# A gated MLP's first pair: both batches' gates first, then the second batch's values directly and the first batch's by Strassen

## The chip, the cores and the metric

The kernel runs on one core of a Trainium2 chip. The metric is the device time of one execution in microseconds. The engines of the core are TensorE (PE; its weight loads are PEld), VectorE (DVE), ScalarE (ACT), GpSimd (POOL) and SyncE (SP), whose queue issues the loads. Each works through its own instructions in order, and semaphores hold one back until another has finished.

## The reference

Clustered attention gives `x` of 1536 tokens (two batches of 768) by 512 features. Two MLPs follow. The change lies in the first sixth of the second one, which has 1536 hidden features:

```python
def _moe_ref(x, w_in, w_out):            # first MLP, 2048 hidden features
    h = x @ w_in
    g = h * (1.0 / (1.0 + np.exp(-h)))
    return (g @ w_out).astype(np.float32)

def _moe2_ref(x, w_gate, w_val, w_out):  # second MLP, 1536 hidden features
    gate = 1.0 / (1.0 + np.exp(-(x @ w_gate)))
    val = x @ w_val
    return (gate * val @ w_out).astype(np.float32)
```

## The kernel before, in words

Every float32 product is made of three matmuls: an operand is split into a high part (ScalarE's `cast`, L62) and the rest (a subtraction, L74, L617 or L769), and high times high, high times low and low times high are summed in PSUM.

**Pairs.** The first MLP runs over 8 pairs of 128-column blocks of its hidden features, the second over 6 (`N2`). For a pair the first product (`w_gate`, `w_val`) is a 2 by 2 block product over halves of the 512 input features and halves of a batch's tokens. `direct` (L779) computes it with 48 matmuls of 128x384 for one batch and one of the two weights. `strassen` (L714) needs seven block products of 6 matmuls each, in the order x, y, z, w, X, v, W, so 42; but it needs sums of weights (`seven`, with the four steps L644 to L647 on GpSimd) and sums of the operand `y` (`sums`: L88, L91, L95 and L99 on VectorE, each with a cast L62 and a subtraction L74), and it combines the products with additions on VectorE (L737, L739, L747, L753, L756).

**Weights.** `converted` (L600 to L609) loads a weight of 64-bit floats into a raw buffer (two in turn, `rp`) and makes it float32 in five steps: ScalarE L605, GpSimd L606, VectorE L607, L608, L609. `weights` starts the conversion two jobs ahead of its use. A raw buffer is free for the load two further on when the last of its steps, L609, has ended. Raw tiles are named `rg`, `rv`, `ru` (gate, value, out), converted ones `cg`, `cv`, `cu`, with pair and half behind (`cv1_0`).

**PSUM.** Banks come from two pools of two buffers, `ppa` and `ppb`. `direct` takes one of each for its two halves `m`, `strassen` takes `ppa` for x and w and `ppb` for y, z and v. A third bank of one pool has to wait until the first has been read.

**Order.** TensorE's order is that of the code (`tc.manual_schedule`). The orders of VectorE, ScalarE and GpSimd come from a scheduler that has the whole program before it, under the limits of `tc.issue_after`.

**The place of the change.** After the first MLP's last product (`mixed`, L829) the first pair of the second MLP is computed directly for both batches, so that Strassen's sums of `y` can be made beside it: `gated_directly(0, 0)` has the gates q and the values r of batch 0, then come the sums of batch 0, `gated_directly(0, 1)`, and the sums of batch 1. `gate` applies the sigmoid on ScalarE (L861), `value` multiplies on VectorE (L865), and `split` casts the result on ScalarE (`ghb`, L62) and subtracts on VectorE (`glb`, L769). Then `out_of(0)` (L887) multiplies pair 0 by `w_out` in six steps of two 128-token blocks and ScalarE copies each bank away (L807). `gated(1, ALL)` follows, by Strassen for both batches at once.

Of the kernel before, what the change touches and what calls it, by code (L numbers as in the profile page):

```python
# [31 lines left out]
def clustered_attention_then_two_mlps(ctx, tc, qT, kT, v, cen, w1i, w1o, w2g, w2v, w2o, out):  # L32
# [633 lines left out]
    def job(key, make, *args):  # L666
        place[key] = len(jobs)
        jobs.append(partial(make, *args))

    def flat(w):  # L670
        return w.rearrange("p k c -> p (k c)")
# [4 lines left out]
            job(("1o", i, e), plain, w1o[i, e], f"o{i}_{e}")  # L676
    for i in range(N2):
        job(("2g", i), seven if i else four, [flat(w2g[2 * i + n]) for n in range(2)], f"g{i}")
        job(("2v", i), seven if i else four, [flat(w2v[2 * i + n]) for n in range(2)], f"v{i}")
        for k in range(2):  # L680
            job(("2o", i, k), plain, flat(w2o[2 * i + k]), f"u{i}_{k}")

# [20 lines left out]
    def temporary(name):  # L703
        return up.tile([P, 2, HS], F32, tag="u", name=name)
# [57 lines left out]
    def split(src, m, at, i, subber):  # L762

        for t in "hl":
            if (i, m, t) not in gs:
                gs[i, m, t] = gp.tile([P, 2, B, HS], R32, tag=f"g{t}{m}", name=f"g{t}{i}_{m}")
        hi, lo = (gs[i, m, t][(slice(None), *at)] for t in "hl")
        cast(nc.scalar, hi, src)
        subber.tensor_tensor(lo, src, hi, op=ALU.subtract)  # L769

    def direct(w, name, take, b):

        for m in range(2):
            o = bank(f"{name}_{b}{m}", (ppa, ppb)[m])
            for h in range(2):
                for r in range(2):
                    for k in range(KQ):
                        for n, (s, t) in enumerate(((0, 0), (0, 1), (1, 0))):
                            nc.tensor.matmul(  # L779
                                o[:, h, 0:HS],  # L780
                                lhsT=w[f"a{m + 1}{r + 1}"][s][:, k, :],
                                rhs=right[b, f"{r + 1}{h + 1}"][t][:, k, :],
                                start=r == 0 and k == 0 and n == 0,
                                stop=r == 1 and k == KQ - 1 and n == 2,
                            )
            take(o[:, :, 0:HS], m, b)
            yield
# [65 lines left out]
        yield from strassen(weights("2g", i), f"g{i}", gate, bs)  # L853
        yield from strassen(weights("2v", i), f"v{i}", value, bs)

    def gated_directly(i, b):
        gates = {}

        def gate(c, m, b):
            gates[m] = temporary(f"g2{i}_{m}_{b}")  # L860
            nc.scalar.activation(gates[m], c, AF.Sigmoid)  # L861

        def value(c, m, b):
            g = gates[m]
            nc.vector.tensor_tensor(g, c, g, op=ALU.mult)  # L865
            split(g, m, (slice(0, 2), b), f"b{i}", nc.vector)

        yield from direct(weights("2g", i), f"q{i}", gate, b)
        yield from direct(weights("2v", i), f"r{i}", value, b)

    oa = acc.rearrange("p d h b s -> p (d h b s)")
    PER = HS // P
# [1 line left out]
    def out_of(i):  # L874
# [1 line left out]
        half = B * S // P // 2  # L876
        pairs = [(t, t + 1) for t in range(0, 2 * half, 2)]
        if i == 0:
            ts = [t for b in range(B) for t in range(2 * half) if t % half // PER == b]
            pairs = [tuple(ts[n : n + 2]) for n in range(0, 2 * half, 2)]  # L880
        oc = oa.rearrange("p (t c) -> p t c", c=NB)
        def products(o, t, u, k):
# [42 lines left out]
    def steps(main, beside=iter(()), n=None):  # L925

        for _ in main:
            next(beside, None)
            if n is not None:
                n -= 1  # L930
                if n == 0:
                    return

    def run(gen):
        for _ in gen:
            pass
# [43 lines left out]
    steps(mixed(N1 - 1, 1), beside)  # L980
    run(beside)
    beside = plain_operands("y", 1)
    steps(gated_directly(0, 0), beside)
    run(beside)
    run(sums("y", 0))
    last("y", 0)
    run(gated_directly(0, 1))
    run(sums("y", 1))
    last("y", 1)
    run(out_of(0))  # L990
    run(gated(1, ALL))
# [59 lines left out]
```

## Time and the profile before

| | us |
|---|---|
| three runs | 798.1, 798.85, 799.65 (median 798.85) |
| profiled execution | 796.14 |
| its span, first to last instruction | 794.3 |
| TensorE busy | 768.8 (97%) |
| VectorE busy | 641.5 (81%) |
| ScalarE busy | 390.9 (49%) |
| GpSimd busy | 399.5 (50%) |

The profiled execution has 1.84 us outside its span and is 2.71 us below the median of the runs. The mean granted clock of TensorE is 0.992 of full speed. The first pair's four direct products take TensorE from 508.60 to 541.88 us of the span, and `out_of(0)` from there to 558.45.

### The profile page before, as it was taken

What the parts mean: (1) busy time and instruction counts of PE and PEld (TensorE: products, weight loads), DVE (VectorE), ACT (ScalarE), POOL (GpSimd) and SP (SyncE); (2) the same over time, 40 slices, a digit from 0 to 9 for tenths busy, and PEclk for the clock granted to TensorE, in tenths of its full rate; (3) what the DMA queues carried; (4) which work ended last, traced back from release to release, by engine and by line L of the source; (5) the groups of instructions that cost most, each with busy time, mean ns of one, the idle gap of its engine ahead of it and who ended that gap; (6) DMA issues with size and microseconds to landing.
All of it is one profiled execution on the core that took longest, in us unless ns stands there. A gap on an engine that the chain in (4) does not pass through costs nothing.

```text
span 794.3 us, 11424 instructions
## 1 busy us (share of the span) xinstructions
PE 768.8 (97%) x4299; PEld 657.1 (83%) x4299; DVE 641.5 (81%) x806; ACT 390.9 (49%) x669; POOL 399.5 (50%) x343
## 2 busy tenths in 40 slices
PE   6999999999998999999999999999999999999996
PEld 3666666766766999989989889998998989899895
DVE  5888887987987899988687778999397896979654
ACT  4665666756765865425335246555532425334120
POOL 3342641781235657756456436346564847748220
PEclk8999999999999999999999999999999999999999
DMA  8874476366321122321121121121121221121004
GB/s 192 212 184 114 124 186 142 114 180 139 95 73 54 54 80 80 133 79 54 66 94 43 64 80 54 65 70 53 54 80 54 80 80 54 54 80 54 1 0 160
DMA packets 25040, 72.07 MB, mean 91 GB/s; under 512 B 4100, under 2 KB 4184, under 8 KB 24984
## 3 DMA queue, kind: packets, MB, share of 16 engines
q1 hardware_dynamic: 24984, 71.33, 30.4%
q8 instruction: 34, 0.56, 0.3%
q14 instruction: 22, 0.18, 0.1%
HBM read 47.87 MB, written 3.19 MB: 64 GB/s over the span
## 4 chain that ended last, share of the span: by engine, by line
PE 76%; DVE 16%; ACT 4%; issue 2%; POOL 1%; DMA 0%; DVEq 0%; ACTq 0%
PE z L887 12%; PE v L457 6%; DVE nm L422 5%; PE s L414 4%; PE h_0x L714 4%; PE h_0w L714 3%; PE y L829 3%; PE g_0w L714 3%; DVE ph L65 3%; PE g_0x L714 2%; PE v_0w L714 2%; PE v_0x L714 2%; PE t L450 2%; PE y_00None L829 2%; PE r L779 2%; PE q L779 2%
## 5 line engine op out<-in xcount | busy, mean ns | idle before, releaser
L427 ACT ACTIVATE e<-s,nm 128x768 f32<-128x768 f32 x96 | 86.5, 902 | 44.4 <-DVE nm L422 40.9
L422 DVE TENSOR_REDUCE nm<-s 128x1 f32<-128x768 f32 x96 | 90.9, 949 | 5.6 <-PE s L414 4.5
L887 PE MATMUL z<-wu,ghb 128*128 128x512 f32 x288 | 89.3, 391 | 0.5 <-DVE acc L809 0.5
L457 PE MATMUL v<-ph,vv 128*64 128x384 f32 x384 | 71.4, 503 | 0.5 <-DVE ph L65 0.5
L414 PE MATMUL s<-ka,qa 128*128 128x384 f32 x192 | 58.7, 387 | 8.1 <-ACT e L427 7.8
L887 PEld LDWEIGHTS z<-wu,ghb 128*128 128x128 f32 x288 | 53.6, 188 | 12.4 <-issue 1.2
L450 PE MATMUL t<-ident,e 128*128 128x128 f32 x384 | 59.0, 277 | 2.1 <-DVE ph L65 1.0
L887 PE MATMUL z<-wu,glb 128*128 128x512 f32 x144 | 56.7, 394 | 0.0
L414 PEld LDWEIGHTS s<-ka,qa 128*128 128x128 f32 x192 | 29.4, 192 | 28.3 <-ACT e L427 17.8
L414 PE MATMUL s<-k,q 128*128 128x384 f32 x192 | 50.7, 345 | 1.0 <-DVE k L334 1.0
L450 PEld LDWEIGHTS t<-ident,e 128*128 128x128 f32 x384 | 44.1, 141 | 8.8 <-issue 3.6
L457 PEld LDWEIGHTS v<-ph,vv 128*64 128x64 f32 x384 | 25.2, 139 | 31.3 <-issue 27.8
L353 POOL TENSOR_SCALAR qq<-qq 128x768 f32<-128x768 f32 x7 | 5.9, 836 | 88.6 <-DMA qq<-in_qT 56.2
L809 DVE TENSOR_TENSOR acc<-z,acc 128x1024 f32<-128x1024 f32 (+1 forms) x31 | 36.3, 1185 | 14.6 <-PE z L887 13.8
L469 DVE TENSOR_TENSOR xf<-v,other 64x384 f32<-64x384 f32 x32 | 17.7, 554 | 34.1 <-ACT other L466 34.0
L62 ACT ACTIVATE ph<-t 128x512 f32<-128x512 f32 x48 | 28.7, 598 | 20.0 <-PE t L450 19.7
L441 PE MATMUL u<-ident,e 128*128 128x128 f32 x192 | 37.0, 276 | 0.8 <-ACT e L427 0.8
L414 PEld LDWEIGHTS s<-k,q 128*128 128x128 f32 x192 | 35.4, 192 | 1.3 <-DVE k L334 1.3
L65 DVE COPY ph<-u 128x512 f32<-128x512 f32 x48 | 32.6, 680 | 1.2 <-PE u L441 1.2
L65 DVE COPY ph<-t 128x512 f32<-128x512 f32 x48 | 32.6, 680 | 0.7 <-PE t L450 0.5
L887 PEld LDWEIGHTS z<-wu,glb 128*128 128x128 f32 x144 | 27.0, 188 | 7.4 <-DVE glb L769 1.8
L829 PE MATMUL y<-gha,wo 128*128 128x384 f32 x128 | 32.8, 334 | 0.0
(627 smaller groups left out, 2160.5 us busy)
## 6 DMA issues: line engine op xcount, KB each, us to landing
ri<-in_w1i SPq DMA_DIRECT2D x16, 512.0 KB, 3.3
ro<-in_w1o SPq DMA_DIRECT2D x16, 512.0 KB, 3.2
ka<-kh SPq DMA_DIRECT2D x32, 192.0 KB, 3.9
rg<-in_w2g SPq DMA_DIRECT2D x12, 512.0 KB, 3.1
rv<-in_w2v SPq DMA_DIRECT2D x12, 512.0 KB, 3.2
ru<-in_w2o SPq DMA_DIRECT2D x12, 512.0 KB, 3.2
qq<-in_qT SPq DMA_DIRECT2D x8, 384.0 KB, 4.9
kk<-in_kT SPq DMA_DIRECT2D x8, 384.0 KB, 6.3
```

The source lines that it names most:

```text
L65: return nc.vector.tensor_copy(o, i)
L414: nc.tensor.matmul(s[:, g, 0:HS], lhsT=a[:, j, i * P : (i + 1) * P], rhs=c[:, j, g * HS : (g + 1) * HS], start=n == 0, stop=n == 1,)
L422: nc.vector.tensor_reduce(nm, s[:, :, 0:HS], axis=AX.XY, op=ALU.max, negate=True)
L427: x = nc.scalar.activation(e, s[:, :, 0:HS], AF.Exp, bias=nm, scale=1.0, accum_out=tots[p][:, n : n + 1])
L441: nc.tensor.transpose(both[:, kt - 4, i % 2, :], e[:, kt * P : (kt + 1) * P], ident)
L450: nc.tensor.transpose(t[:, kt, :], e[:, kt * P : (kt + 1) * P], ident)
L457: m = nc.tensor.matmul(o[(L, U)[kt % 2]], lhsT=vv[:, j, kt, :], rhs=ring[:, kt, g * G : (g + 1) * G], start=n < 2, stop=n >= NT - 2,)
L714: nc.tensor.matmul(o[:, b, 0:HS], lhsT=w[a][s][:, k, :], rhs=right[b, q][t][:, k, :], start=start and k == 0 and n == 0, stop=k == KQ - 1 ...
L779: nc.tensor.matmul(o[:, h, 0:HS], lhsT=w[f"a{m + 1}{r + 1}"][s][:, k, :], rhs=right[b, f"{r + 1}{h + 1}"][t][:, k, :], start=r == 0 and k ...
L809: nc.vector.tensor_tensor(z, o, z, op=ALU.add)
L829: nc.tensor.matmul(o[:, d, 0:width], lhsT=s[:, d, k, :], rhs=t[:, c], start=k == 0 and m == 0, stop=k == 1 and m == 2,)
L887: nc.tensor.matmul(o[:, a, :], lhsT=s[:, q * P : (q + 1) * P], rhs=r, start=k == 0 and m == 0, stop=k == 1 and m == 2, skip_group_check=True,)
```

## The change

The gates of both batches come first, directly; then the values of batch 1, directly; then the values of batch 0 by Strassen. So the sums of batch 0 have to be there before its values are computed. `out_of(0)` takes batch 1's blocks of tokens ahead of batch 0's. `seven(..., all_four=True)` makes the four direct blocks and the sums of the first value weight. The sums of batch 1 are issued behind the last subtraction of `split` (`ends[2]`).

```diff
--- before.py
+++ after.py
@@ -676,7 +676,7 @@
             job(("1o", i, e), plain, w1o[i, e], f"o{i}_{e}")
     for i in range(N2):
         job(("2g", i), seven if i else four, [flat(w2g[2 * i + n]) for n in range(2)], f"g{i}")
-        job(("2v", i), seven if i else four, [flat(w2v[2 * i + n]) for n in range(2)], f"v{i}")
+        job(("2v", i), seven, [flat(w2v[2 * i + n]) for n in range(2)], f"v{i}", i == 0)
         for k in range(2):
             job(("2o", i, k), plain, flat(w2o[2 * i + k]), f"u{i}_{k}")
 
@@ -766,7 +766,7 @@
                 gs[i, m, t] = gp.tile([P, 2, B, HS], R32, tag=f"g{t}{m}", name=f"g{t}{i}_{m}")
         hi, lo = (gs[i, m, t][(slice(None), *at)] for t in "hl")
         cast(nc.scalar, hi, src)
-        subber.tensor_tensor(lo, src, hi, op=ALU.subtract)
+        ends[2:] = [subber.tensor_tensor(lo, src, hi, op=ALU.subtract)]
 
     def direct(w, name, take, b):
 
@@ -853,20 +853,28 @@
         yield from strassen(weights("2g", i), f"g{i}", gate, bs)
         yield from strassen(weights("2v", i), f"v{i}", value, bs)
 
-    def gated_directly(i, b):
+    def first_gated(i):
+
         gates = {}
 
         def gate(c, m, b):
-            gates[m] = temporary(f"g2{i}_{m}_{b}")
-            nc.scalar.activation(gates[m], c, AF.Sigmoid)
+            gates[m, b] = temporary(f"g2{i}_{m}_{b}")
+            nc.scalar.activation(gates[m, b], c, AF.Sigmoid)
 
         def value(c, m, b):
-            g = gates[m]
+            g = gates[m, b]
             nc.vector.tensor_tensor(g, c, g, op=ALU.mult)
             split(g, m, (slice(0, 2), b), f"b{i}", nc.vector)
 
-        yield from direct(weights("2g", i), f"q{i}", gate, b)
-        yield from direct(weights("2v", i), f"r{i}", value, b)
+        def by_halves(c, m, h, bs, inside):
+            g = gates[m, bs.start][:, h : h + 1]
+            nc.vector.tensor_tensor(g, c, g, op=ALU.mult)
+            split(g, m, (h, bs), f"b{i}", nc.vector)
+
+        yield from direct(weights("2g", i), f"q{i}", gate, 0)
+        yield from direct(weights("2g", i), f"q{i}", gate, 1)
+        yield from direct(weights("2v", i), f"r{i}", value, 1)
+        yield from strassen(weights("2v", i), f"r{i}", by_halves, slice(0, 1))
 
     oa = acc.rearrange("p d h b s -> p (d h b s)")
     PER = HS // P
@@ -876,7 +884,7 @@
         half = B * S // P // 2
         pairs = [(t, t + 1) for t in range(0, 2 * half, 2)]
         if i == 0:
-            ts = [t for b in range(B) for t in range(2 * half) if t % half // PER == b]
+            ts = [t for b in reversed(range(B)) for t in range(2 * half) if t % half // PER == b]
             pairs = [tuple(ts[n : n + 2]) for n in range(0, 2 * half, 2)]
         oc = oa.rearrange("p (t c) -> p t c", c=NB)
         def products(o, t, u, k):
@@ -980,12 +988,14 @@
     steps(mixed(N1 - 1, 1), beside)
     run(beside)
     beside = plain_operands("y", 1)
-    steps(gated_directly(0, 0), beside)
+    now = first_gated(0)
+    steps(now, beside, 2)
     run(beside)
     run(sums("y", 0))
     last("y", 0)
-    run(gated_directly(0, 1))
-    run(sums("y", 1))
+    run(now)
+    with tc.issue_after(ends[2].ins):
+        run(sums("y", 1))
     last("y", 1)
     run(out_of(0))
     run(gated(1, ALL))
```

The instructions move on the engines as follows. Names carry a running number at the end, which means nothing.

**GpSimd, end of the first MLP.** `cv0` is pair 0's value weight, `wv0` what is made of it, `sv0` its sums, `h7` and `gla7` the first MLP's last pair. Before, from the step L606 of `cu0_0`:

```order
L606 TENSOR_SCALAR cu0_0_5207<-cu0_0_5207 128x512
L617 TENSOR_TENSOR wv01_5093<-cv0_1_5087,wv01_5093 128x512
L617 TENSOR_TENSOR wv00_5082<-cv0_0_5076,wv00_5082 128x512
L769 TENSOR_TENSOR gla7_1_4944<-h7_1d_5001,gha7_1_4943 128x384
L606 TENSOR_SCALAR cu0_1_5278<-cu0_1_5278 128x512
L617 TENSOR_TENSOR wu0_0_5213<-cu0_0_5207,wu0_0_5213 128x512
L606 TENSOR_SCALAR cg1_0_5506<-cg1_0_5506 128x512
L606 TENSOR_SCALAR cg1_1_5514<-cg1_1_5514 128x512
```

And in the change:

```order
L606 TENSOR_SCALAR cu0_0_5218<-cu0_0_5218 128x512
L644 TENSOR_TENSOR sv0_5093<-cv0_1_5084 128x256
L646 TENSOR_TENSOR sv0_5093<-cv0_0_5076,cv0_1_5084 128x256
L645 TENSOR_TENSOR sv0_5093<-sv0_5093,cv0_0_5076 128x256
L647 TENSOR_TENSOR sv0_5093<-cv0_0_5076,sv0_5093 128x256
L617 TENSOR_TENSOR wv0a_5090<-cv0_0_5076,wv0a_5090 128x512
L769 TENSOR_TENSOR gla7_1_4944<-h7_1d_5001,gha7_1_4943 128x384
L617 TENSOR_TENSOR wv0s_5098<-sv0_5093,wv0s_5098 128x512
L617 TENSOR_TENSOR wv0t_5101<-sv0_5093,wv0t_5101 128x512
L606 TENSOR_SCALAR cu0_1_5369<-cu0_1_5369 128x512
L617 TENSOR_TENSOR wv0b_5104<-cv0_1_5084,wv0b_5104 128x512
L617 TENSOR_TENSOR wu0_0_5224<-cu0_0_5218,wu0_0_5224 128x512
```

Four steps on `sv0` stand ahead of the first value weight's split, and there are four splits L617 of `wv0` for two.

**VectorE, around the last step of `cv1_0`.** `yt` are batch 0's sums of `y`; `g20_0_1` and `g20_1_1` are the two halves of batch 1's gates, `r0_10` and `r0_11` the banks of its values. Before:

```order
L609 SCALAR_TENSOR_TENSOR cv1_0_5545<-rv1_0_5543,cv1_0_5545 128x512
L88 TENSOR_TENSOR yt10_5353<-acc_58 128x768
L91 TENSOR_TENSOR yt20_5355<-acc_58,yt10_5353 128x768
L607 TENSOR_SCALAR cv1_1_5553<-cv1_1_5553 128x512
L95 TENSOR_TENSOR yt40_5360<-yt20_5355,acc_58 128x768
L99 TENSOR_TENSOR yt30_5365<-acc_58 128x768
L608 SCALAR_TENSOR_TENSOR cv1_1_5553<-rv1_1_5551,cv1_1_5553 128x512
L74 TENSOR_TENSOR yt20_5357<-yt20_5355,yt20_5357 128x768
L865 TENSOR_TENSOR g20_0_0_5241<-r0_00_5287,g20_0_0_5241 128x768
L74 TENSOR_TENSOR yt40_5362<-yt40_5360,yt40_5362 128x768
L609 SCALAR_TENSOR_TENSOR cv1_1_5553<-rv1_1_5551,cv1_1_5553 128x512
```

And in the change:

```order
L74 TENSOR_TENSOR yt30_5307<-yt30_5305,yt30_5307 128x768
L609 SCALAR_TENSOR_TENSOR cv1_0_5568<-rv1_0_5566,cv1_0_5568 128x512
L607 TENSOR_SCALAR cv1_1_5576<-cv1_1_5576 128x512
L608 SCALAR_TENSOR_TENSOR cv1_1_5576<-rv1_1_5574,cv1_1_5576 128x512
L609 SCALAR_TENSOR_TENSOR cv1_1_5576<-rv1_1_5574,cv1_1_5576 128x512
L866 TENSOR_TENSOR g20_0_1_5338<-r0_10_5378,g20_0_1_5338 128x768
L769 TENSOR_TENSOR glb0_0_5405<-g20_0_1_5338,ghb0_0_5404 128x2x384
L607 TENSOR_SCALAR cu1_0_5678<-cu1_0_5678 128x512
L608 SCALAR_TENSOR_TENSOR cu1_0_5678<-ru1_0_5676,cu1_0_5678 128x512
L866 TENSOR_TENSOR g20_1_1_5365<-r0_11_5408,g20_1_1_5365 128x768
L609 SCALAR_TENSOR_TENSOR cu1_0_5678<-ru1_0_5676,cu1_0_5678 128x512
L737 TENSOR_TENSOR r0_0u2_5439<-r0_0y_5447,r0_0u2_5439 128x384
```

The step L609 of `cv1_0` stood ahead of batch 0's sums, and now stands behind all eight of their operations; the multiplication of `r0_11`, which frees its bank, stands behind the steps L607 and L608 of `cu1_0`.

**ScalarE, the same place.** Before, from the step L605 of `cv1_1`:

```order
L605 ACTIVATE cv1_1_5553<-rv1_1_5551 128x512
L861 ACTIVATE g20_1_0_5271<-q0_01_5246 128x768
L62 ACTIVATE yt20_5357<-yt20_5355 128x768
L605 ACTIVATE cu1_0_5655<-ru1_0_5653 128x512
L62 ACTIVATE yt40_5362<-yt40_5360 128x768
L62 ACTIVATE yt30_5367<-yt30_5365 128x768
L62 ACTIVATE ghb0_0_5313<-g20_0_0_5241 128x2x384
```

And in the change:

```order
L605 ACTIVATE cv1_1_5576<-rv1_1_5574 128x512
L862 ACTIVATE g20_1_1_5365<-q0_11_5340 128x768
L62 ACTIVATE wg1a_5543<-cg1_0_5529 128x512
L62 ACTIVATE wv1d_5596<-cv1_1_5576 128x256
L605 ACTIVATE cu1_0_5678<-ru1_0_5676 128x512
L62 ACTIVATE ghb0_0_5404<-g20_0_1_5338 128x2x384
L735 ACTIVATE r0_0u2_5439<-r0_0x_5438 128x384
```

The step L605 of `cu1_0` now stands directly ahead of the cast `ghb` of the first values; before, three rows lay between it and the cast, none of which waits for the load of `ru1_0`.

**ScalarE, `out_of(0)`.** `z0_3` is the bank of blocks 3 and 4 and so on, `yt..1` are batch 1's sums. Before:

```order
L62 ACTIVATE yt11_5500<-yt11_5483 128x768
L62 ACTIVATE wv1s_5567<-sv1_5562 128x512
L62 ACTIVATE ghb0_1_5346<-g20_1_1_5425 128x2x384
L807 ACTIVATE acc_58<-z0_0_5503 128x1024
L807 ACTIVATE acc_58<-z0_2_5583 128x2x512
L807 ACTIVATE acc_58<-z0_7_5597 128x1024
```

And in the change:

```order
L62 ACTIVATE yt11_5523<-yt11_5506 128x768
L807 ACTIVATE acc_58<-z0_3_5526 128x1024
L62 ACTIVATE yt21_5510<-yt21_5508 128x768
L605 ACTIVATE cg2_0_5917<-rg2_0_5915 128x512
L62 ACTIVATE yt41_5515<-yt41_5513 128x768
L62 ACTIVATE yt31_5520<-yt31_5518 128x768
L807 ACTIVATE acc_58<-z0_5_5606 128x2x512
L807 ACTIVATE acc_58<-z0_10_5620 128x1024
L807 ACTIVATE acc_58<-z0_0_5634 128x1024
L807 ACTIVATE acc_58<-z0_2_5648 128x2x512
```

The copies of the banks had batch 1's casts ahead of them, and now the second copy stands behind all of these.

## Rows read from the trace of the kernel before

**Rows 1.** The page, part 1: busy time and its share of the span by engine.

```profile
PE 768.8 (97%) x4299; PEld 657.1 (83%) x4299; DVE 641.5 (81%) x806; ACT 390.9 (49%) x669; POOL 399.5 (50%) x343
```

**Rows 2.** Windows: the first two products; us, then busy time (instructions) by engine.

```profile
core 0: us, PE busy (x) PEld busy (x) DVE busy (x) ACT busy (x) POOL busy (x), PEclk, DMA share, GB/s
508.60:525.24 16.64, 16.64 (x98) 16.64 (x97) 16.57 (x18) 9.85 (x14) 10.41 (x10) 1.00 0.27 94
```

**Rows 3.** Timeline of TensorE: start us, duration us, what it does.

```profile
508.60 8.48 PE L779 MATMUL q<-y,wg 128*128 128x384 f32 x48
...
541.88 0.63 PE L887 MATMUL z<-wu,ghb 128*128 128x512 f32 x2
...
551.44 0.61 PE L887 MATMUL z<-wu,ghb 128*128 128x512 f32 x2
...
552.28 0.63 PE L887 MATMUL z<-wu,ghb 128*128 128x512 f32 x2
```

**Rows 4.** Timeline of VectorE, 517 to 544 us.

```profile
517.50 1.22 DVE L608 SCALAR_TENSOR_TENSOR cv<-rv,cv 128x512 int32<-128x512 int32 x1
518.76 1.11 DVE L609 SCALAR_TENSOR_TENSOR cv<-rv,cv 128x512 int32<-128x512 int32 x1
519.79 1.49 DVE L88 TENSOR_TENSOR yt<-acc 128x768 f32<-128x768 f32 x1
...
522.49 0.41 DVE L607 TENSOR_SCALAR cv<-cv 128x512 int32<-128x512 int32 x1
522.83 0.94 DVE L95 TENSOR_TENSOR yt<-yt,acc 128x768 f32<-128x768 f32 x1
523.70 0.95 DVE L99 TENSOR_TENSOR yt<-acc 128x768 f32<-128x768 f32 x1
...
533.14 0.68 DVE L608 SCALAR_TENSOR_TENSOR cu<-ru,cu 128x512 int32<-128x512 int32 x1
...
543.38 0.95 DVE L865 TENSOR_TENSOR g<-r,g 128x768 f32<-128x768 f32 x1
```

**Rows 5.** Timeline of SyncE's queue; an issue.

```profile
519.95 0.33 SPq L600 DMA_DIRECT2D ru<-in_w2o  x1
```

**Rows 6.** Timeline of ScalarE, 523 to 553 us.

```profile
523.36 0.66 ACT L605 ACTIVATE cu<-ru 128x512 f32<-128x512 f32 x1
...
527.43 0.85 ACT L62 ACTIVATE ghb<-g 128x768 fp32r<-128x768 f32 x1 [1.90 <-DVE g L865]
...
549.78 2.84 ACT L807 ACTIVATE acc<-z 128x1024 f32<-128x1024 f32 x3
```

**Rows 7.** Timeline of GpSimd, 514 to 545 us.

```profile
514.51 1.38 POOL L644 TENSOR_TENSOR sg<-cg 128x256 f32<-128x256 f32 x1 [2.35 <-DVE cg L609]
515.85 0.92 POOL L646 TENSOR_TENSOR sg<-cg,cg 128x256 f32<-128x256 f32 x1
516.73 1.45 POOL L645 TENSOR_TENSOR sg<-sg,cg 128x256 f32<-128x256 f32 x1
...
519.28 1.19 POOL L647 TENSOR_TENSOR sg<-cg,sg 128x256 f32<-128x256 f32 x1
...
534.52 1.31 POOL L617 TENSOR_TENSOR wg1s<-sg,wg1s 128x512 fp32r<-128x512 f32 x1 [4.20 <-ACT wg1s L62]
535.79 1.74 POOL L617 TENSOR_TENSOR wg1t<-sg,wg1t 128x512 fp32r<-128x512 f32 x1
...
542.65 1.97 POOL L617 TENSOR_TENSOR wv1a<-cv,wv1a 128x512 fp32r<-128x512 f32 x1 [0.88 <-ACT wv1a L62]
```

**Rows 8.** Timeline of VectorE in pair 1, its longest idle time nearby in brackets.

```profile
562.90 0.96 DVE L737 TENSOR_TENSOR g_0u<-g_0y,g_0u 128x768 f32<-128x768 f32 x1 [8.14 <-PE g_0y L714]
```

**Rows 9.** Timeline of TensorE: two waits, in brackets, early in the kernel and later.

```profile
12.35 0.50 PE L327 MATMUL pt<-identb,oh 128*64 128x128 bf16 x6 [2.73 <-DVE oh L319]
...
283.44 0.44 PE L829 MATMUL y<-gla,wo 128*128 128x384 f32 x1 [1.64 <-DVE gla L769]
```

**Rows 10.** A window at the start of the kernel; PEclk stands behind the five engines.

```profile
14.00:20.50 6.50, 5.35 (x18) 4.42 (x19) 4.83 (x11) 2.96 (x6) 0.00 (x0) 0.50 1.04 204
```

## The prediction

> **What bounds the kernel now.** I read the page first: TensorE is busy for 768.8 of the 794.3 us of the span, 97%; the next engine is VectorE with 81% [rows 1]. So a microsecond can be won only where TensorE gets less to do, and is lost wherever it is made to wait. Then I read the stretch of the change by windows. While TensorE computes the first two products (508.60 to 525.24), it is busy for all 16.64 us, but VectorE is busy for 16.57 of them, ScalarE for 9.85 and GpSimd for 10.41 [rows 2]. The reader is to see that VectorE is full exactly where the change gives it deadlines. Third, the timeline of TensorE gives the schedule to be kept: gates begin at 508.60, `out_of(0)` at 541.88 [rows 3]; between them lie four products of 48 matmuls, 33.28 us, so 8.32 us each and 173.3 ns a matmul.
>
> **What it removes.** Strassen has 42 matmuls for 48 of the same 128x384 form: 6 x 173.3 ns = 1.04 us less. In `out_of(0)` one group of three matmuls takes 0.84 us (551.44 to 552.28), because a `glb` comes late; the first groups run from 541.88 to 551.44 with 14 groups at 0.68 [rows 3]. Batch 1's last `glb` is no longer made at that place, so 0.16 us more may be won. Together **-1.20 us**, the whole of what there is to win.
>
> **What it adds: a deadline behind a long chain.** TensorE's new times without a wait: gates to 525.24, batch 1's values to 533.56, then x, y, z, w, X, v, W at 1.04 us each, `out_of(0)` at 540.84. Strassen's y and z both take `ppb`, which has two buffers; z, due at 508.60 + 3 x 8.32 + 2 x 1.04 = 535.64, needs the bank of `r0_11`, so it waits for the multiplication L866 of `r0_11` on VectorE. By the new orders that stands behind: L609 of `cv1_0` (it frees the raw buffer), the load of `ru1_0`, ScalarE's L605 of `cu1_0`, ScalarE's `ghb` behind it, VectorE's `glb`, L607 and L608 of `cu1_0`, and the multiplication itself. Nothing in this chain is part of the product; it is the order of the queues that ties them together.
>
> The chain's length from rows: L609 ended at 518.76 + 1.11 = 519.87 [rows 4], SyncE issued the load at 519.95 [rows 5], L605 of `cu` began at 523.36 [rows 6]: 3.49 us. Behind it come L605 0.66 and `ghb` 0.85 [rows 6], `glb`, taken as the 0.94 of a 128x768 operation, L607 0.41, L608 0.68, and L866 as L865's 0.95 [rows 4]. That is 7.98. The steps on one engine begin before the recorded end of the last one (522.83 to 523.70 is 0.87 for a row of 0.94 [rows 4]); with 0.07 off at four seams it is 7.7 us. So z is on time if L609 of `cv1_0` ends by 535.64 - 7.7 = **527.9**.
>
> When will it? In before it ends at 519.87. The change puts batch 0's eight operations of `sums` ahead of it: the first two take 2.70 us (519.79 to 522.49), the other six 0.87 each, 5.22 [rows 4]. 519.87 + 7.92 = **527.8**. So without any other effect the deadline is met with 0.1 us to spare. That is a coincidence of two sums, and what decides is the rest:
>
> GpSimd gets four sums of weights (L644 to L647) and two splits L617 more, ahead of this place. The same four took 1.38, 0.92, 1.45 and 1.19, 4.94 us; splits took 1.31 and 1.74, 3.05 for two [rows 7]: 8.0 us. What does this do to VectorE? Beside GpSimd's steps from 514.51 on, L608 took 1.22, where it takes 0.68 later, when GpSimd stands still (533.14); L609, of the same form, 1.11; L88 took 1.49, where L99 takes 0.95 [rows 4, 7]: 1.51 us lost in the 3.8 from 517.50 to where these end, 0.40 us for each of GpSimd's. An operation that reads PSUM is not slowed: L865 took 0.95 at 543.38, in the middle of a split [rows 4, 7]. Of the 53 operations of VectorE from `cv0_1` to L609 of `cv1_0` in the new order 14 read PSUM, so some 0.7 of the time can be slowed: 8.0 x 0.40 x 0.7 = 2.2 us. The bounds are 0 (the work falls into gaps and beside PSUM reads) and all of it, with the shortest rows 4 x 0.92 + 2 x 1.31 = 6.3. I take 2.2, because it is what the nearest rows give.
>
> The Trainium skill ("SBUF — State Buffer", section "Who interferes with whom") calls the port pair that VectorE and GpSimd share an exclusive lock: an operation with two inputs in SBUF and a GpSimd operation that reads SBUF exclude each other for a whole instruction, and the loser stands still. The rows of both engines [rows 4, 7] agree with it on which operations suffer, not on standing still for the whole time; what the sum would be by it is given with the rivals.
>
> ScalarE gets two casts more (`wv0s`, `wv0t`), which wait for GpSimd's sums and stand ahead of casts that VectorE's `gla` needs. Each costs less than the 0.85 of `ghb`; bounds 0 and 1.7, and I take 0.3, since ScalarE is busy for little more than half the time [rows 2]. So L609 ends at 527.8 + 2.2 + 0.3 = 530.3, and **TensorE waits 2.4 us at z** (bounds 0, and 7.9 with both terms at their upper ends).
>
> **Second place.** Batch 1's sums of `y` now begin when the last split of batch 0 is done, and ScalarE's copy of `z0_5` stands behind their last cast. The sixth bank, `z0_7`, needs the bank of `z0_5`, and without waits starts at 540.84 + 5 x 2.73 = 554.5 (12 matmuls at the pace of 541.88 to 551.44 [rows 3] are 2.73). The last product W ends at 540.8; behind it come some five short operations on VectorE and ScalarE in turn and ScalarE's queue, so the sums start at 544 to 546. L88 to L99 with one subtraction took 5.7 us (519.79 to 524.6, and 0.87 [rows 4]), the cast 0.85, the copy 0.95 (2.84 for three) [rows 6]: 551.5 to 553.5, all of it later together with TensorE. So there are 1 to 3 us to spare, of which GpSimd's sums for `cv1` can take most. Bounds 0 and 1.0; I take **0.5**.
>
> **At nothing.** VectorE's extra halves for batch 0 (additions, four multiplications and splits for two) lie behind z, and the backlog of conversions that they push back is absorbed in pair 1, where VectorE stands idle for 8.14 us until 562.90 [rows 8]. If that cover were gone, the backlog would show as a wait at `g_0`; the price would be the two splits and multiplications more, about 2 us. The issue order of loads is unchanged; only `ru1_0` comes later, which is in the chain above.
>
> **Sum.** -1.04 - 0.16 + 2.4 + 0.5 = +1.7 us. On the profiled execution, 796.14, that is 797.8. The median of the runs lies 2.71 above it; I assume this for the change as well: 798.85 + 1.7 = **800.6 us**.
>
> **The rivals.**
> - *The deadline is met.* GpSimd's extra work lies beside VectorE for nothing, L609 ends by 527.9, and only the gain is left: 798.85 - 1.20 = 797.7. This is the case on the other side. For it: the two sums meet within 0.1 us, and ScalarE and GpSimd have free time. Against it: VectorE has 0.07 us of slack in 16.64 and operations half again as long beside GpSimd. It decides when the cost of the added work is below 0.1 to 0.2 us; up to about 1.2 it breaks even.
> - *VectorE stands still for all of GpSimd's added work*, 6.3 us by the rows above: z waits 6.2, and with the second place the time is 798.85 - 1.2 + 6.2 + 0.5 = 804.4. By the Trainium skill's lock on the shared ports ("SBUF — State Buffer", as above) the time would be near that. Against it: 0.40 in the rows, not 1.
> - *The wait lowers TensorE's clock.* After 2.73 us of waiting until 12.35 [rows 9], and thin work, the granted clock was 0.50 from 14.0 to 20.5 [rows 10], its lower level, 1.2 GHz, for 2.4. After 1.64 us at 283.44 matmuls went on at their pace [rows 9]. A wait of 2.4 lies between them. 6.5 us at half the clock lose 3.2: 803.8. Against it: the work before and behind it is dense here. The Trainium skill ("TensorE: Matmul & The Clock Gate", "Part 1: The HAM clock gate") has the clock go down after an idle stretch; no row here shows a wait of this size in dense work.
> - *The second place is the main one*: no wait at z, but 1 us or more at `z0_7`; 798.6 or so, and no change.
>
> **How the numbers follow.** A measurement of this kernel tells about 0.2%, 1.6 us, from no change, so slower begins at 800.45 and faster at 797.25. My forecast (a wait at z between 1 and 4 us, clock kept) gets 0.50, and by its size splits into 0.19 within the bound and 0.31 slower. The deadline met, or the second place alone, gets 0.20 (0.17 no change, 0.03 faster, as it wins 1.2 at most). The clock gets 0.14, VectorE standing still 0.14, both slower; 0.02 is left for a gain of another kind, counted half as faster and half as no change. That gives faster 0.04, same 0.37, slower 0.59. The range goes from the deadline met, 797.6, to the two expensive rivals, 804.2; likely enough half of each of these lies outside.
>
> **What would show it.** In the profile after: one wait of TensorE at L714 for VectorE's L866, near 535.6, of 2 to 3 us, and a smaller one at L887 for ScalarE's L807; L609 of `cv` behind the eight sums, near 530; ScalarE's L605 of `cu` 3.5 us behind it; operations on SBUF alone of 1.1 to 1.5 us beside GpSimd between 490 and 515. A TensorE without a wait in 508 to 560 would refute me, as would a wait that begins at another instruction. The prediction would also be wrong if L609 of `cv1_0` ended by 528 though GpSimd did its 8 us more.

## The result, and the profile after

The change takes 805.13 us (median of 8 runs, 802.86 to 807.93), the kernel before 798.63 (8 runs): a ratio of 1.0075, 95% interval 1.0055 to 1.0095, so 4.4 to 7.6 us slower. Slower had the largest chance and is what came, but the time lies above the range's upper end of 804.2: the wait came where it was forecast and was nearly twice as long, and TensorE's clock fell on top of it.

The profiled execution took 804.5 us, with a span of 802.7. TensorE's busy time rose by 1.3 us [rows 1] though it has six matmuls fewer, which already says that some of them ran slowly. The page after, part 1:

```profile
PE 770.1 (96%) x4293; PEld 658.8 (82%) x4293; DVE 649.9 (81%) x815; ACT 392.9 (49%) x674; POOL 404.4 (50%) x349
```

TensorE, from the end of batch 1's values to pair 1 (timeline: start us, duration us; idle time before, and what ended it, in brackets). It answers to [rows 3]:

```profile
536.31 1.20 PE L714 MATMUL r_0x<-y,wv0a 128*128 128x384 f32 x6
537.35 1.21 PE L714 MATMUL r_0y<-yt,wv0s 128*128 128x384 f32 x6
542.81 2.29 PE L714 MATMUL r_0z<-yt,wv0t 128*128 128x384 f32 x6 [4.25 <-DVE g L866]
544.90 2.12 PE L714 MATMUL r_0w<-yt,wv0s 128*128 128x384 f32 x6
546.82 1.87 PE L714 MATMUL r_0x<-y,wv0a 128*128 128x384 f32 x6
...
549.57 1.20 PE L714 MATMUL r_0w<-y,wv0t 128*128 128x384 f32 x6
550.61 0.63 PE L895 MATMUL z<-wu,ghb 128*128 128x512 f32 x2
...
564.90 0.73 PE L895 MATMUL z<-wu,ghb 128*128 128x512 f32 x2 [0.49 <-ACT acc L807]
...
567.76 2.27 PE L714 MATMUL g_0x<-y,wg1a 128*128 128x384 f32 x12
```

The first gate began at 511.35 here and at 508.60 before [rows 3]. The lag of 2.75 us comes from the attention part far ahead of the change: the first MLP already began 2.67 us later (254.75 for 252.08). It differs between executions of one program (256.78 when the change was profiled once more), so from here on I compare stretches, each from one profiled execution: from the first gate to pair 1's first matmul it was 49.85 us before (508.60 to 558.45) and is 56.41 (511.35 to 567.76), **6.56 more**. From there to the last matmul both take 229.5. So all of the loss lies in these rows, and it adds up:

| step | forecast | measured |
|---|---|---|
| six matmuls fewer | -1.04 | -1.04 (z due at 538.39, 27.04 behind the first gate, as counted) |
| wait at z | +2.4 | +4.42 (538.39 to 542.81) |
| products z, w, X, v, W | 0 | +2.60 (542.81 to 550.61 is 7.80, not 5 x 1.04) |
| `out_of(0)`, with `z0_7` | -0.16 + 0.5 | +0.58 (17.15 instead of 16.57) |
| sum | +1.7 | +6.56 |

The third line is the clock. Products z and w have rows nearly twice as long as x and y. Windows (us, busy time and instructions of PE, PEld, DVE, ACT, POOL, then the granted clock):

```profile
540.00:541.00 1.00, 0.00 (x0) 0.00 (x0) 1.00 (x2) 0.22 (x1) 0.00 (x0) 1.00 0.01 4
541.00:542.00 1.00, 0.00 (x0) 0.00 (x0) 0.97 (x3) 0.00 (x0) 0.00 (x0) 0.72 0.00 0
542.00:543.00 1.00, 0.19 (x1) 0.19 (x2) 1.00 (x2) 0.21 (x1) 0.00 (x0) 0.50 0.00 0
...
547.00:548.00 1.00, 1.00 (x5) 1.00 (x4) 0.91 (x2) 0.63 (x1) 0.23 (x1) 0.50 0.00 0
548.00:549.00 1.00, 1.00 (x6) 1.00 (x6) 0.48 (x2) 0.28 (x1) 1.00 (x1) 0.87 0.00 0
```

The clock is still full some 2.5 us into the wait, falls to 0.50 (1.2 GHz for 2.4) before the wait ends, and is back from the window 548 to 549 on, after more than 5 us of dense work: z and w run at half speed throughout, the second X partly.

Why was z late? VectorE's timeline, from the first sum of batch 0 to the multiplication that frees z's bank; it answers to [rows 4]:

```profile
520.24 0.95 DVE L88 TENSOR_TENSOR yt<-acc 128x768 f32<-128x768 f32 x1
521.22 1.38 DVE L91 TENSOR_TENSOR yt<-acc,yt 128x768 f32<-128x768 f32 x1
522.52 1.50 DVE L74 TENSOR_TENSOR yt<-yt,yt 128x768 fp32r<-128x768 f32 x1
523.94 1.49 DVE L95 TENSOR_TENSOR yt<-yt,acc 128x768 f32<-128x768 f32 x1
525.35 1.49 DVE L99 TENSOR_TENSOR yt<-acc 128x768 f32<-128x768 f32 x1
526.77 1.49 DVE L74 TENSOR_TENSOR yt<-yt,yt 128x768 fp32r<-128x768 f32 x1
528.77 1.51 DVE L607 TENSOR_SCALAR cv<-cv 128x512 int32<-128x512 int32 x1 [0.51 <-POOL cv L606]
530.20 0.94 DVE L74 TENSOR_TENSOR yt<-yt,yt 128x768 fp32r<-128x768 f32 x1
531.07 1.10 DVE L608 SCALAR_TENSOR_TENSOR cv<-rv,cv 128x512 int32<-128x512 int32 x1
532.09 2.04 DVE L74 TENSOR_TENSOR yt<-yt,yt 128x768 fp32r<-128x768 f32 x1
534.05 0.68 DVE L609 SCALAR_TENSOR_TENSOR cv<-rv,cv 128x512 int32<-128x512 int32 x1
...
539.87 0.96 DVE L769 TENSOR_TENSOR glb<-g,ghb 128x768 fp32r<-128x768 f32 x1 [2.48 <-ACT ghb L62]
...
541.81 0.95 DVE L866 TENSOR_TENSOR g<-r,g 128x768 f32<-128x768 f32 x1
```

And GpSimd in the same stretch (timeline), which answers to [rows 7]:

```profile
520.40 1.38 POOL L644 TENSOR_TENSOR sg<-cg 128x256 f32<-128x256 f32 x1 [3.61 <-DVE cg L609]
521.74 1.47 POOL L646 TENSOR_TENSOR sg<-cg,cg 128x256 f32<-128x256 f32 x1
523.16 1.45 POOL L645 TENSOR_TENSOR sg<-sg,cg 128x256 f32<-128x256 f32 x1
524.58 1.45 POOL L617 TENSOR_TENSOR wg1d<-cg,wg1d 128x256 fp32r<-128x256 f32 x1
525.99 1.46 POOL L647 TENSOR_TENSOR sg<-cg,sg 128x256 f32<-128x256 f32 x1
```

The reader is to see the two engines in step: from 521.2 to 528 each starts a new operation about every 1.42 us, and VectorE's take 1.38 to 1.50 where L95 and L99 took 0.94 and 0.95 before [rows 4]. There GpSimd stood still up to the middle of L99 (timeline, before):

```profile
524.09 1.03 POOL L606 TENSOR_SCALAR cu<-cu 128x512 f32<-128x512 f32 x1 [2.33 <-ACT cu L605]
```

GpSimd's sums are slowed as well. In pair 1 of the kernel before, with VectorE not reading two operands from SBUF beside them, the same two steps take 0.74 and 0.75 (timeline, before):

```profile
567.27 0.74 POOL L644 TENSOR_TENSOR sg<-cg 128x256 f32<-128x256 f32 x1 [4.31 <-DVE cg L609]
567.97 0.75 POOL L646 TENSOR_TENSOR sg<-cg,cg 128x256 f32<-128x256 f32 x1
```

These sums `sg` of pair 1's gate weight were in the kernel before too, but ran beside other steps. L609 of `cv1_0` ends at 534.73, 23.38 behind the first gate.

Last, the link by which a weight's conversion holds up a product. SyncE's queue, then ScalarE (timelines):

```profile
534.81 2.11 SPq L600 DMA_DIRECT2D ru<-in_w2o  x2
```

```profile
538.45 0.66 ACT L605 ACTIVATE cu<-ru 128x512 f32<-128x512 f32 x1 [1.48 <-DMA ru<-in_w2o]
539.01 0.83 ACT L62 ACTIVATE ghb<-g 128x768 fp32r<-128x768 f32 x1
```

The load is issued as soon as L609 has freed the raw buffer, ScalarE waits for it, and the cast `ghb` stands behind. From L609's end to z it is 542.81 - 534.73 = 8.08 us; forecast 7.7.

### The profile page after: what moved, and what is told of

It reads as the page before. It is cut to its first block, busy times and chain, and to the rows that moved or that the text cites. A ratio compares the mean times of both kernels' runs of the same rounds, so it can differ in the third digit from the quotient of the medians.

```text
span 802.7 us, 11434 instructions
## 1 busy us (share of the span) xinstructions
PE 770.1 (96%) x4293; PEld 658.8 (82%) x4293; DVE 649.9 (81%) x815; ACT 392.9 (49%) x674; POOL 404.4 (50%) x349
## 4 chain that ended last, share of the span: by engine, by line
PE 70%; DVE 21%; ACT 3%; issue 3%; POOL 1%; DMA 0%; DVEq 0%; ACTq 0%; POOLq 0%; SPq 0%
PE z L895 10%; PE v L457 6%; PE s L414 5%; DVE nm L422 5%; PE h_0x L714 4%; PE h_0w L714 3%; PE g_0w L714 3%; DVE ph L65 2%; PE t L450 2%; PE g_0x L714 2%; PE v_0w L714 2%; PE v_0x L714 2%; PE y_00None L829 2%; PE y_20None L829 2%; PE y_11None L829 2%
```

## Experiments

The theory: weight sums that run beside the sums of `y`, and conversions whose order ties them to the multiplication that frees z's bank, make the wait, and the wait makes the clock fall. Rivals were that the new order of products by itself costs the time, that the chain is not what z waits for, and that the slow products have another cause. Each was compared with the kernel before on its own chip. "Stretch" is as above, 49.85 us before and 56.41 in the change, each from one profiled execution.

| run | ratio (95%) | first gate, pair 1 | stretch |
|---|---|---|---|
| e1_order_alone | 0.9989 (0.9966 to 1.0012) | 514.20, 563.84 | 49.64 |
| e2_sums_alone | 1.0059 (1.0030 to 1.0088) | 515.62, 569.43 | 53.81 |
| e3_late_z | 1.0042 (1.0013 to 1.0070) | 516.21, 569.53 | 53.32 |
| e4_out_weight_later | 1.0029 (1.0006 to 1.0052) | 511.47, 564.69 | 53.22 |
| e5_values_first | 1.0022 (0.9998 to 1.0047) | 513.03, 564.91 | 51.88 |
| e6_no_sums | 0.9996 (0.9978 to 1.0014) | 515.67, 566.50 | 50.83 |
| e7_busy_wait | 1.0068 (1.0036 to 1.0101) | 513.38, 567.75 | 54.37 |
| e8_copies_first | 1.0012 (0.9990 to 1.0034) | 513.41, 562.92 | 49.51 |
| e9_conversions_last | 0.9981 (0.9952 to 1.0010) | 516.58, 565.18 | 48.60 |
| e10_value_weight_sooner | 1.0056 (1.0033 to 1.0079) | 510.55, 566.75 | 56.20 |
| e11_change_again | 1.0075 (1.0043 to 1.0106) | 513.82, 569.59 | 55.77 |

**e1_order_alone.** The change with batch 0's values direct, and so without the first value weight's sums:

```diff
-        job(("2v", i), seven, [...], f"v{i}", i == 0)
+        job(("2v", i), seven if i else four, [...], f"v{i}")
...
-        yield from strassen(weights("2v", i), f"r{i}", by_halves, slice(0, 1))
+        yield from direct(weights("2v", i), f"r{i}", value, 0)
```

> The new order of products with batch 0's values computed directly and pair 0's value weight as before. My theory (the wait at z, and the lower clock behind it, come from the deadline that Strassen's third bank sets) gives no wait of TensorE in pair 0 above 0.5 us and the time of the kernel before within 0.2% (797.0 to 800.2 us). The rival that the order itself costs, since VectorE gets batch 0's sums ahead of batch 1's values either way, gives a wait of 2 us or more and over 800.6 us.

No wait in the stretch, and 49.64 us of it. L609 of `cv1_0` ended 10.85 behind the first gate. So the order gates, gates, values by itself costs nothing, and it does not by itself put `cv1_0` behind the sums.

**e2_sums_alone.** The kernel before, with the sums of the first value weight made and not used:

```diff
-        job(("2v", i), seven if i else four, [...], f"v{i}")
+        job(("2v", i), seven, [...], f"v{i}", i == 0)
```

> The kernel before, with only the sums of pair 0's first value weight made on GpSimd and ScalarE, and not used. My theory gives no wait of TensorE in pair 0 above 0.5 us and the time of before within 0.2%; in the trace L609 of cv1_0 ends later by 2 us or more against the gates' start, since GpSimd's eight microseconds slow VectorE. The rival that GpSimd's added work is what costs TensorE its time gives 801 us or more.

TensorE's two waits in the stretch (timeline):

```profile
557.71 0.70 PE L887 MATMUL z<-wu,ghb 128*128 128x512 f32 x2 [0.44 <-DVE g L865]
562.95 0.50 PE L887 MATMUL z<-wu,glb 128*128 128x512 f32 x1 [2.78 <-DVE glb L769]
```

Without any change on TensorE the stretch is 3.96 us longer, all of it in `out_of(0)`, and these waits are 3.2 of it. L609 of `cv1_0` ended 23.63 behind the first gate, as late as in the change. My expectation that the sums would be hidden fell. With e1 it shows which part of the change brings the late L609: the work for GpSimd, with the order of the queues that the scheduler makes of it, and not the order of TensorE's products.

**e3_late_z.** The change with Strassen's products in the order x, w, X, y, z, v, W, so that z is due 2.08 us later:

```diff
-        yield from strassen(weights("2v", i), f"r{i}", by_halves, slice(0, 1))
+        yield from strassen(weights("2v", i), f"r{i}", by_halves, slice(0, 1), "xwXyzvW")
```

> The change with Strassen's products in the order x, w, X, y, z, v, W, so that z is due two products (2.08 us) later; the queues of the other engines stay as they were up to there. From the first gate to pair 1's first matmul the kernel before took 49.85 us and the change 56.41. My theory: the bank of r0_11 comes when it came, so the wait at z is 4.4 - 2.1 = 2.3 us, and the stretch 54.3 us if the clock falls as well, 51.7 if a wait of 2.3 us leaves it. The rival (z waits for its own operand or Strassen's order costs by itself) leaves the wait at 4 us.

TensorE's waits (timeline):

```profile
544.81 1.32 PE L714 MATMUL r_0x<-y,wv0a 128*128 128x384 f32 x6 [1.20 <-ACT r_0u L735]
...
547.36 1.34 PE L714 MATMUL r_0z<-yt,wv0t 128*128 128x384 f32 x6 [0.17 <-DVE g L866]
...
550.17 1.32 PE L714 MATMUL r_0v<-yt,wv0b 128*128 128x384 f32 x6 [1.46 <-DVE r_0u L737]
```

I expected 2.3 us of wait at z. z hardly waits, but X waits for ScalarE's copy and v for VectorE's addition, which stand in the same queues behind the same conversions. The wait is cut into 1.20, 0.17, 1.46 and 0.43 (at W). It is not shorter: the seven products end 4.6 us behind their time without a wait (541.17 to 553.07, for 7.28 us), where the change's one wait was 4.42. No piece took the clock: the granted clock stayed at 1.00, and every product has its 1.2 to 1.3 us. So the order of products moves and spreads the wait, and most of what the stretch is shorter than in the change (3.09) is the clock's part.

**e4_out_weight_later and e5_values_first.** In e4 the conversion of `cu1_0` is issued on VectorE behind the multiplication L866 of `r0_11` and on ScalarE behind that value's cast, so that the chain's end is untied. In e5 the conversions of pair 1's value weight, `cv1_0` and `cv1_1`, are held behind L866 as well (`marks["mul"]` is that multiplication, `marks["cast"]` its cast):

```diff
+    LATER = {place["2o", 1, 0]: ("mul", "cast"), place["2v", 1]: ("mul",)}   # e4: without the second
...
-                with tc.issue_after((ends if c > AHEAD else begin)[0].ins):
+                with ExitStack() as held:
+                    held.enter_context(tc.issue_after((ends if c > AHEAD else begin)[0].ins))
+                    for mark in LATER.get(c, ()):
+                        held.enter_context(tc.issue_after(marks[mark].ins))
```

> The change with only the conversion of pair 1's first out weight later: on ScalarE behind the casts of batch 1's values and on VectorE behind the multiplication of r0_11; pair 1's value weight stays ahead of both. My theory: the load of ru1_0 and three conversion steps leave the chain, and cast, glb and multiplication stay: the wait at z falls from 4.25 to 1.5 to 2.0 us, the clock stays at 1.00, and the stretch from the first gate to pair 1's first matmul takes 51.0 to 52.0 us (56.41 in the change). The rival (the load is no part of the chain, VectorE is simply that late) leaves the wait above 3 us.

> The change, with the conversions of pair 1's value weight and first out weight queued on VectorE behind the multiplication of r0_11, and ScalarE's part of the latter behind the casts of batch 1's values. My theory gives no wait at z (r0_11's bank free at once), a granted clock of 1.00 throughout pair 0, and 805.1 - 4.25 - 2.6 = 798.3 us, 797.5 to 799.5. A rival (the backlog of conversions that is pushed back returns as a wait in out_of(0) or pair 1) gives 800 us or more with a wait there. If the sums of y themselves were late, z or x would still wait.

TensorE in e4, and then in e5 (timelines; the kernels' lines are shifted by 4 or 5):

```profile
540.31 1.31 PE L718 MATMUL r_0z<-yt,wv0t 128*128 128x384 f32 x6 [1.64 <-DVE g L870]
```

```profile
562.06 0.73 PE L900 MATMUL z<-wu,ghb 128*128 128x512 f32 x2 [2.09 <-ACT acc L811]
```

In e4 L609 is as late as in the change (23.39 behind the gate), but z waits 1.64 instead of 4.25: so most of what z waited for is the tie through the load of `ru1_0` and ScalarE. Two waits for copies, 0.88 and 0.92, follow in `out_of(0)`, so the stretch is longer than the 51.0 to 52.0 that I expected. In e5 z does not wait at all; W waits 0.61, and 2.09 of the time come back at `z0_7`. In both the granted clock stayed at 1.00. The prediction's second place is thus real, and grows when the first is relieved: what VectorE owes in the stretch is put off, not removed.

**e6_no_sums.** The change, with the four GpSimd sums of pair 1's gate weight left out and the weight's own halves split in their place (so pair 1's gates are made with other weights). The scheduler then puts the steps of `cu1_0` behind L866, as in e4, and e4 is what this run is compared with:

```diff
+        if name != "g1":
             sub(t[:, 0], a21, a22, op=ALU.add)
...
```

> The change without the four sums of pair 1's gate weight on GpSimd (the weight's own halves are split in their place, so pair 1's gates come out wrong); VectorE and ScalarE have the order of the run with the later out weight up to the multiplication of r0_11. My theory (the sums of y lose 3 to 4 us because GpSimd's sums run beside them): the sums of y take 0.95 us each again for most, L609 of cv1_0 ends 3 us earlier against the first gate (23.4 us in the change), and no wait at z above 0.5 us remains. The rival (the sums are late by their place in the queue alone) leaves L609 at 23 us and a wait of 1.5 to 2 us.

VectorE's L99, and TensorE's only wait in the products (timelines):

```profile
529.03 0.95 DVE L99 TENSOR_TENSOR yt<-acc 128x768 f32<-128x768 f32 x1
```

```profile
548.97 1.34 PE L718 MATMUL r_0w<-y,wv0t 128*128 128x384 f32 x6 [1.93 <-DVE r_0d L760]
```

L99 takes 0.95 again where it took 1.49, L609 ends 21.06 behind the gate, 2.3 earlier than in e4, and the wait at z is gone. This is what my sum left out: 2.3 us of VectorE's time beside sums that exist in both kernels. A wait of 1.93 at W stays, and so do slow steps beside what GpSimd still does.

**e7_busy_wait.** The change, with the product y computed five times over in the same bank, so that TensorE is busy while it would wait for z:

```diff
+                    o["y"] = bank(f"{name}y")
+                    for _ in range(4):
+                        run(o["y"], "s2", "t2")
```

> The change, with Strassen's product y computed five times in the same bank, so that TensorE works through 24 needless matmuls (4.16 us) where it waited. If the slow products z, w and X come from the clock that fell in the wait, the clock stays at 1.00, z starts when it did, and the time is 805.1 - 2.6 = 802.5 us (801.7 to 803.3). If they are slow because an operand or a bank comes late, nothing is won: 805 us or more.

TensorE (timeline), and the granted clock (windows):

```profile
539.38 5.36 PE L714 MATMUL r_0y<-yt,wv0s 128*128 128x384 f32 x30
544.78 1.31 PE L714 MATMUL r_0z<-yt,wv0t 128*128 128x384 f32 x6
545.93 1.20 PE L714 MATMUL r_0w<-yt,wv0s 128*128 128x384 f32 x6
```

```profile
545.00:548.00 3.00, 3.00 (x18) 3.00 (x18) 2.48 (x5) 1.24 (x2) 0.12 (x1) 1.00 0.45 150
```

z begins 31.40 us behind the first gate, in the change 31.46: the wait is filled, not shortened. z and w now take 1.31 and 1.20 instead of 2.29 and 2.12, at a clock of 1.00. The five products take 5.31 us for 7.80, so 2.5 of the 2.60 us of the third line were the clock's, and it fell because TensorE stood idle. `out_of(0)` gives 0.5 of them back (17.66 for 17.15; its wait is 0.89 instead of 0.49). The stretch shows it; in whole runs 2 us do not separate this kernel from the change.

**e8_copies_first.** e5 with three things more: `out_of(0)` begins ahead of batch 1's sums in the program, these sums are issued behind its second copy (`marks["copy"]`, which frees the bank of `z0_5`), and pair 1's out weights are converted behind the sums:

```diff
+    now = out_of(0)
+    steps(now, n=2)
+    with tc.issue_after(ends[2].ins), tc.issue_after(marks["copy"].ins):
...
+    run(now)
```

> The run with values first, and besides ScalarE's casts of batch 1's sums behind the copy of z0_5, and pair 1's out weights converted behind these sums. My theory: neither the wait at z nor those at W (0.61) and z0_7 (2.09) remain, and the stretch from the first gate to pair 1's first matmul is that of before less Strassen's six matmuls and the late glb: 48.7 us, at most 49.3; the time 0.1 to 0.2% under the kernel before. The rival: the pushed-back sums make a wait in pair 1 (at g_0y or g_0z), and nothing is won.

This kernel leaves out a dependency: the first two copies write `acc` from 550.97 and 552.85 on, and the sums read it only from 554.58 on, so batch 1's sums are made of overwritten tokens. It is of use for its times alone. Stretch 49.51, with one wait of 0.61 at W and none at `z0_7`; waits of 0.40 and 1.56 follow in `out_of(1)`, and from the first gate to the last matmul it takes 281.12 us, 1.81 more than before. So `z0_7` waits only for what stands ahead of ScalarE's copies, and the time comes back further on.

**e9_conversions_last and e10_value_weight_sooner.** The mechanism of e4, for all conversions from `cv1` to `cu1_1`: in e9 they are issued behind the last subtraction (and for `cu1`, the last cast) of batch 1's sums. In e10 `cv1` already behind Strassen's addition L756:

```diff
+    LATER = {c: ("sub", "sum cast") if c > place["2v", 1] else ("sub",)   # e10: ("d",) for cv1
+             for c in range(place["2v", 1], place["2o", 1, 1] + 1)}
```

> The change with all conversions of pair 1's value weight and out weights queued on VectorE behind batch 1's sums, and ScalarE's part of the out weights behind their casts. My theory (every wait of pair 0 is VectorE's backlog of conversions put ahead of work that is due sooner): no wait of TensorE above 0.3 us at z, W and z0_7, and 48.7 to 49.1 us from the first gate to pair 1's first matmul (49.85 before, 56.41 in the change). From there to the end it took 235.85 us before; the theory has room for the conversions there, so 235 to 236. The rival: the backlog comes back in pair 1, as a wait at v_0x or v_0y for wv1 or in out_of(1), and that part takes 237 us or more.

> The run with the conversions last, but with pair 1's value weight converted on VectorE behind Strassen's sum d, in gaps that it had there; the out weights stay behind batch 1's sums. My theory: z and W keep their time; batch 1's sums start up to 2.5 us later, which is about what the copy of z0_5 had to spare, so 48.6 to 49.6 us from the first gate to pair 1's first matmul; the load of ru1_0 comes 8 to 10 us earlier, and the two waits for wg2t in pair 2 (1.6 us) go. From the first gate to the last matmul it then takes 278.0 to 279.0 us, where the kernel before took 279.3 and the run with the conversions last 279.5. The rival (GpSimd's sums for pair 1's values slow the sums of y as they did in the run with values first) brings 1.5 us or more of waiting at z0_2 or z0_7.

TensorE in e9, where z began without a wait; then in e10 the wait at the sixth bank, and a window that begins near its end:

```profile
543.62 1.20 PE L721 MATMUL r_0z<-yt,wv0t 128*128 128x384 f32 x6
```

```profile
561.46 1.22 PE L903 MATMUL z<-wu,ghb 128*128 128x512 f32 x2 [3.17 <-ACT acc L814]
```

```profile
561.00:565.00 4.00, 3.54 (x8) 2.81 (x9) 1.71 (x3) 4.00 (x6) 1.13 (x2) 0.50 0.00 0
```

In the stretch e9 has the whole gain and nothing else: 48.60 us, 1.25 less than before, as -1.04 and -0.16 had it, though GpSimd makes all its sums. But two waits of 0.79 and 0.76 for weights come in pair 2, and from the first gate to the last matmul it takes 279.54 us where the kernel before takes 279.31 and the change 285.88. In whole runs it is not told from the kernel before. e10 missed: with `cv1` sooner, its weight sums run beside batch 1's sums of `y`, the same contention in another place; `out_of(0)` begins with a wait of 1.31, and one of 3.17 at the sixth bank took the clock to 0.50.

**e11_change_again.** The change itself once more, for the spread of the wait and the clock.

> The change as it is, on the same chip as the run beside it. All theories: a ratio of 1.0055 to 1.0095 to the kernel before, a wait of 4.2 to 4.4 us at z, the clock at half for about 7 us behind it, and 56.4 us from the first gate to pair 1's first matmul. If the wait or the clock's fall differed from execution to execution, this profile would show another one.

TensorE (timeline), and windows:

```profile
545.22 1.81 PE L714 MATMUL r_0z<-yt,wv0t 128*128 128x384 f32 x6 [4.19 <-DVE g L866]
546.83 2.12 PE L714 MATMUL r_0w<-yt,wv0s 128*128 128x384 f32 x6
```

```profile
544.00:545.00 1.00, 0.00 (x0) 0.00 (x0) 1.00 (x2) 0.00 (x0) 0.00 (x0) 1.00 0.00 0
545.00:546.00 1.00, 0.79 (x4) 0.79 (x5) 1.00 (x3) 0.81 (x1) 0.00 (x0) 0.89 0.00 0
546.00:547.00 1.00, 1.00 (x5) 1.00 (x4) 1.00 (x2) 0.04 (x1) 0.00 (x0) 0.50 0.02 8
```

The wait repeats to 0.06 us; the five products took 6.87, so the clock cost 1.67 here and 2.60 in the first profile. Here it was still full when the wait ended (1.00 from 544 to 545) and fell only after z had begun. The wait is the program's, the clock's price varies with the execution.

## Why the prediction was wrong

- **Bound, gain.** Right: TensorE loses one for one, and the six matmuls gave 1.04.
- **Place and chain.** Right: one wait at L714's z for L866, through L609, the load, L605, `ghb` and `glb`. Its length was 8.08 for 7.7; 0.4 of the wait. e4, which cuts the chain at `cu1_0`, confirms it: 1.64 of the 4.25 are left.
- **The failed step: "the other six 0.87 each".** I priced the eight sums that move ahead of L609 at 7.92, with rows in which GpSimd stood still for most of them [rows 4], and counted as slowed only what GpSimd gets in addition. Their rows after add up to 11.28; less 0.07 at each of eight seams that is 10.7, and a wait of 0.51 for GpSimd's L606 comes with them: 3.3 us more. A moved operation gets the neighbour of its new place, and there the sums `sg` of pair 1's gate weight run without a break. e6 takes these sums away and wins 2.3 of it back.
- **"4.94 and 3.05 ... 2.2 us".** Too dear. VectorE reached the first sum 8.89 us behind the gate. Before it was 11.19 with `cv1_0`'s three steps ahead (0.95, 1.22 and 1.11, some 3.1), so 8.1: the added work cost 0.8 for the 2.5 that I took with ScalarE's 0.3. The six steps themselves took 6.96 us for my 8.0. The rate of 0.40 us lost for each of GpSimd's was right for rows of this kind (1.49 - 0.95 in 1.42 is 0.38); it was charged in the wrong stretch. Together -1.7 and +3.3 make L609 1.7 later (23.38 for 21.7), and with the chain's 0.4 the wait 4.42 for 2.4.
- **The clock, a rival with 0.14.** True, and its price of 3.2 near the 1.7 to 2.6 measured. I had set it against my forecast as another case; it follows from it as soon as the wait is large enough, so an error of 2 us in the wait cost 4.6. The Trainium skill ("TensorE: Matmul & The Clock Gate", "Part 1: The HAM clock gate") has the clock fall after idling, and the rows of the change (0.50 behind 4.25 us), e10 (0.50 behind 3.17) and e11 (0.50 behind 4.19) agree, as does e7, where the idling is filled and the clock stays at 1.00.
- **VectorE standing still, a rival with 0.14.** Its 6.2 us of wait did not come. The Trainium skill's lock ("SBUF — State Buffer", "Who interferes with whom") fits the rows in that the two engines go in step, each holding up the other. It is also nearer to them than my "0.40 in the rows, not 1" says. Undisturbed, such operations start every 0.87 us on VectorE [rows 4] and every 0.70 on GpSimd (567.27 to 567.97, above), 1.57 for one of each; the turn takes 1.42. So VectorE loses 0.55 us to a step that alone takes GpSimd 0.70. I had divided by rows of GpSimd that VectorE had already lengthened, and my "shortest" row of 0.92 was one of them.
- **Second place.** Right that it exists, and close in size, 0.49 for 0.5, which is partly luck: TensorE came there 7 us late, and with less of that lateness it is 0.84 (e11) and 0.89 (e7). e5 shows that it is 2.09 when the first is relieved.
- **"At nothing".** Right: pair 1 and what follows take as long as before.
- **What stays open.** Why the scheduler puts all eight sums ahead of `cv1_0` once GpSimd has the added work (e1 against e2) was seen in its order, not traced to a rule of it.

## What to carry to other kernels

Price a moved operation by rows that have the neighbours of its new place, above all where VectorE and GpSimd both work in SBUF, and follow each in-order queue for what comes to stand ahead of the step with the deadline: here a weight that nobody needed yet held the bank that TensorE needed. A wait of TensorE is not priced by its length alone; add the slow products behind it when the wait is as long as those at which this kernel's clock fell. A relieved wait can come back at the next deadline (e4, e5 and e8 in `out_of`, e9 in pair 2's weights): count a gain only over the whole way to the last matmul, where e9's 1.25 us were gone.

## What the runs showed of the hardware

- In dense work, waits of 1.64 (e4), 1.93 (e6), 2.09 (e5) and 2.78 us (e2) left the granted clock at 1.00. Waits of 3.17 (e10) and 4.2 (the change, twice) took it to 0.50, in the change once before the wait had ended and once only after it. The same wait cost 2.60 in one execution and 1.67 in another. Each of the other lengths was seen in one profile only, so no rule for the lengths between follows.
- Beside GpSimd's operations VectorE's operations with two inputs in SBUF take 1.38 to 1.50 us for 0.95, some 2.04, and L607, with one input, 1.51 for 0.41 [rows 4]; GpSimd's sums take 1.38 to 1.47 for 0.74. One that reads PSUM stays at 0.95 in the middle of a split (L865 at 543.38 before [rows 4, 7]).
- The attention part far ahead of the change moved the first gate between 508.60 and 516.58 us in these profiles (the first MLP began between 252.08 and 259.95), more than the change costs, which is why stretches decide here and not spans.
